# Attention with a routed expert layer: raw q, k in idle weight buffers, loads two iterations sooner, a third batch's choice on GpSimd

## The chip, the cores and the metric

The kernel runs on one core of one Trainium2 chip. The metric is device time in microseconds (us). Three runs of the kernel before gave 502.47, 502.87 and 504.84; the median is 502.87.

## The reference, cut to what matters

```python
# q, k, v: [4 batches, 12 heads, 448 rows, 64]
scores = q @ k.T / sqrt(64);  scores = where(row < col, -1e9, scores)
attn = softmax(scores);  x = (attn @ v), rearranged to [1792 tokens, 768]
logits = x @ w_gate + modality_bias[modality_id]          # 8 experts
e = argmax(logits, axis=1);  gate = softmax(logits)[e]
out[token] = gate * (relu(x[token] @ w1[e]) @ w2[e])       # w1 768x1024, w2 1024x768
```

All of it is float32. The expert of a token is chosen by its logits, so attention is computed nearly exactly: a float32 operand is split into a high part (rounded to the matmul's format) and a low part (the rest), and products are summed from the parts.

## The kernel before, in words

The program has one instruction stream per engine, written out in a fixed order. Each engine runs its stream in order, and waits at an instruction until what it needs is there. All plain transfers are issued by the sync engine (SP), also in order; GpSimd (POOL) issues the indirect ones. So the order of the text is the order in each queue.

**Attention** is a software pipeline over 48 heads (`iteration(n)`, L1079, n = 0 to 47). In iteration n TensorE (PE) makes the scores of head n (`st_scores`, banks `sa` and `sb`, one set), transposes the probabilities of head n-2, multiplies those of head n-3 with v (bank `ot`, one) and combines four earlier heads (bank `x`). VectorE (DVE) first adds the output of head n-4 (`ut`, L365), then normalises rows (`ltp`, L412, and `row`, L422), reads the scores of head n (`p`, L280), and last makes the low part `pl` (L321) of the transposed head n-2. ScalarE (ACT) does the exponentials (L290), the high part `ph` (L320), and copies. The next scores can only start when DVE has read the banks of the last, and the next product with v when DVE has done `ut` and `pl`.

**Raw q, k.** Two heads form a pair m. `load_qk(m)` loads 448 KB of raw q and k; POOL makes the high and low parts (`split_qk`, L194 and L195, in iteration 2m-4; `split_kl`, L200 and L202, in iteration 2m-3); SP moves them into stacked operands with four transfers (`stack_qk`, L211 and L212, iteration 2m-3); PE uses them from iteration 2m on. Before, the raw tile comes from a pool of two buffers, and the load stands at the end of iteration 2m-6. Pairs 0 to 2 are loaded whole at the start into parts of the six weight buffers `raw1[0..5]` (`first_view`).

**Rows and routing.** The normalised rows of a batch lie in four `row` buffers (one for each of four row tiles of 64, 128, 128 and 128 rows) and are stored to DRAM (`x_store`, L434). After a batch's last group (iterations 19, 31, 43 for batches 0 to 2) `after_batch` puts its routing into later iterations: `logits` and `top` on DVE, `ties` (L460 to L462), `first_tie` (L465, DVE), `choice` (L469, L470), `places` on PE, ranks, and four indirect writes of eight bytes per token into tables (L501, POOL). `ties` and `choice` are on POOL for batches 0 and 1, on DVE for 2 and 3. `later(n, f)` runs f after the scores of iteration n, `before(n, f)` ahead of them, `soon(n, f)` after the transposes.

**The first expert block.** From the counts of two batches the fullest expert is chosen (`first_slot`, iteration 38). In iterations 42 and 43 SP reads the tokens' ids from the tables (`pre_ids`, L718, four transfers each); `fetch_x` (L728, L729 on DVE, then the gather L730 on POOL) stands behind the scores of iterations 44 and 45. Its six weight blocks (512 KB each) are loaded by `start_w1` (L665) in iterations 42, 43, 44, 45, 46, 46, and POOL splits three of them in iterations 45 to 47 (`w1_chunk`, L673 and L674), after each of which SP loads a block of w2 into the same buffer.

**The expert layer** follows, with PE on matmuls nearly all of the time (L749 to L751).

Of the kernel before, what the change touches and what calls it, by code (L numbers as in the profile page):

```python
# [21 lines left out]
def attention_moe(  # L22
# [162 lines left out]

    def load_qk(m):
        b, j = divmod(m, H // 2)
        raw[m] = t = R([128, 2, S], F32, "raw")
        nc.sync.dma_start(out=t, in_=qk[b, j])

    def split_qk(m):
# [27 lines left out]
        stk.append([t[:, a] for a in range(2)])  # L219

    def first_view(m, c):
        k = 3 * m + c
        return raw1[k % K1][:, k // K1 * S:k // K1 * S + S]

    def first_load(m):
        nc.sync.dma_start(out=first_view(m, 2), in_=qk[0, m, :, 1])
# [154 lines left out]
    def st_comb(gr, i, x=None):  # L381
        b, u = divmod(gr, NG)
        q0, n = QT[i]
        if u == 0:
            xrow[b, i] = row()
            if i == 0:
                lt_all[b] = lts[b % 2]
                P.tensor_scalar(
                    out=lts[b % 2][:, :, H, :], in0=mb[:, b], scalar1=1.0, scalar2=0.0, op0=ALU.mult, op1=ALU.add
                )  # L390
        if x is None:
            x = bank("x")
        for j in range(GH // 2):
            nc.tensor.matmul(
                x[:, j * 2 * XW:(j + 1) * 2 * XW], lhsT=ots(gr, j)[:, q0:q0 + 128],
                rhs=wi[:, u * (GH // 2) + j].rearrange("p a c -> p (a c)"), start=True, stop=True,
            )
        cx[gr, i] = V, x
# [41 lines left out]

    def route(b):
        lg = sm([128, NTL, E], "lg")
        G = V if b >= B - 2 else P
        m = sm([128, NTL], "m")
        m2 = sm([128, NTL], "m2")
        oh = sm([128, NTL, E], "oh", BF16)
        pe = pes[b % 2]
        pc = sm([128, NP + E], "pc")
        sl = sls[b % 2]
        si = sm([128, NTL], "si", I32)  # L450
        zs = sm([128, NTL], "zs")

        def logits():
            V.tensor_reduce(out=lg, in_=lt_all.pop(b).rearrange("p t h e -> p t e h"), axis=AX, op=ALU.add)

        def top():
            V.tensor_reduce(out=m, in_=lg, axis=AX, op=ALU.max)

        def ties():
            G.tensor_tensor(out=lg, in0=lg, in1=wide(m), op=ALU.subtract)  # L460
            G.tensor_scalar(out=eq[:, :, 0:E], in0=lg, scalar1=0.0, scalar2=0.0, op0=ALU.is_equal, op1=ALU.add)
            G.tensor_tensor(out=eq[:, :, 0:E], in0=eq[:, :, 0:E], in1=e8v, op=ALU.mult)  # L462

        def first_tie():
            V.tensor_reduce(out=m2, in_=eq, axis=AX, op=ALU.max)  # L465

        def choice():
            ev = eq[:, :, 0:E]
            G.tensor_tensor(out=ev, in0=ev, in1=wide(m2), op=ALU.subtract)  # L469
            G.tensor_scalar(out=oh, in0=ev, scalar1=0.0, scalar2=0.0, op0=ALU.is_equal, op1=ALU.add)  # L470

        def places():
            prev = rt[b - 1][0][:, NP:] if b else ebase
            ohf = oh.rearrange("p t e -> p (t e)")
            pos = bank("x")
            nc.tensor.matmul(
                pos[:, 0:NP + E].rearrange("p (t e) -> p t e", e=E), lhsT=onesf,
                rhs=eb(prev, NTL + 1)[0:1], start=True, stop=False,
            )
            nc.tensor.matmul(pos[:, 0:NP], lhsT=upper, rhs=ohf, start=False, stop=False)  # L480
            for j in range(1, NTL + 1):
                nc.tensor.matmul(
                    pos[:, j * E:NP + E], lhsT=ones, rhs=ohf[:, 0:NP + E - j * E], start=False, stop=(j == NTL)
                )
            A.activation(out=pc, in_=pos[:, 0:NP + E], func=AF.Copy)
            A.activation(out=pe[:, :, 0:E], in_=lg, func=AF.Exp)
            rt[b] = (pc, si)

        def slots():
            G.tensor_tensor(  # L490
                out=sl[:, :, 0:E], in0=pc[:, 0:NP].rearrange("p (t e) -> p t e", e=E), in1=oh, op=ALU.mult
            )
            V.tensor_reduce(out=zs, in_=pe, axis=AX, op=ALU.add)

        def ranks():
            V.tensor_reduce(out=si, in_=sl, axis=AX, op=ALU.max)
            V.reciprocal(out=ent[:, b, :, 1].bitcast(F32), in_=zs)

        def scatter(ts=range(NTL)):
            for i in ts:  # L500
                P.indirect_dma_start(  # L501
                    out=tables[i][:, :], out_offset=bass.IndirectOffsetOnAxis(ap=si[:, i:i + 1], axis=0),
                    in_=ent[:, b, i, :], in_offset=None, bounds_check=NROW - 1, oob_is_err=False,
                )

        choose = ((1, logits), (1, top), (2, ties), (-3, first_tie), (3, choice))
        return choose, places, (slots, ranks), scatter

    def eb(a, x):
# [365 lines left out]
    with tc.manual_schedule():  # L875
        for m in range(2):
            first_load(m)
        load_v(0)
        first_load(2)
        nc.sync.dma_start(out=modi, in_=mod)  # L880
        nc.sync.dma_start(
            out=bias_sb.rearrange("p m o e -> p (m o e)"),
# [67 lines left out]
        def later(n, f):  # L950
            todo.setdefault(n, []).append(f)
# [62 lines left out]
                    P.tensor_tensor(out=mbv, in0=mbv, in1=mbt, op=ALU.add)  # L1014

        e0 = []
        W1AT = (11, 12, 13, 14, 15, 15)

        def start_w1(k):
            if k == 0:  # L1020
# [6 lines left out]
        def after_batch(b, n):  # L1027
            st = route(b)
            if b == B - 1:
                return st  # L1030
            choose, places, rank, scatter = st
            for j, f in choose:
                later(n + j, f) if j > 0 else before(n - j, f)
            last = b == B - 2
            soon(n + 4, places)
            for j, f in enumerate(rank, 1):
                (later if j % 2 else before)(n + 5 + j // 2, f)
            for i in range(NTL):
                later(n + 7 + (2 * i, i // 2, 0)[b], lambda i=i: scatter([i]))
            if b == 1:  # L1040
                later(n + 6, first_expert)
                before(n + 7, first_slot)
                for j, f in enumerate((first_shift, first_base, first_tri, first_order)):
                    later(n + 9 + j, f)
                for t in range(NPRE):
                    later(n + 11 + t, lambda t=t: pre_ids(t))
                    later(n + 13 + t, lambda t=t: fetch_x(0, 2 * S, t))
                for k in range(K1):
                    later(n + W1AT[k], lambda k=k: start_w1(k))

# [28 lines left out]
        def iteration(n):  # L1079
            if n % 2 == 1 and 5 < n + 3 < NHEAD:  # L1080
                stack_qk((n + 3) // 2)
            if n == 1:
                load_v(1)
            if n and n % GH == 0 and n // GH + 1 < B * NG:
                load_v(n // GH + 1)
            gr, i = divmod(n - 2 * GH, GH)
            comb = 0 <= gr < B * NG
            if 0 <= n - 4 < NHEAD:
                st_out(n - 4)
            if comb:  # L1090
                st_move(gr, i)
                st_norm(gr, i)
                b, u = divmod(gr, NG)
                if u == NG - 1:
                    later(n + 1, lambda i=i: x_store(b, i))
                    if i == NTL - 1:
                        after_batch(b, n)
            run_todo((n,))
            if n in (2, 3):
                st_trans(n - 2)  # L1100
            if n < NHEAD:
                st_scores(n)
            run_todo(n)
            if n == 0:
                split_vh(0)
                split_vl(0)
            if n % 2 == 1 and 5 < n + 3 < NHEAD:
                split_kl((n + 3) // 2)
            if n % 2 == 0 and 5 < n + 4 < NHEAD:
                split_qk((n + 4) // 2)  # L1110
            if n % GH == 1 and n > GH:
                st_sums(n // GH - 1, P)
            if n % GH == RECAT and n > GH:
                st_rec(n // GH - 1)
            if 0 <= n - 1 < NHEAD:
                st_exp(n - 1)
            if 0 <= n - 2 < NHEAD:
                if n > 3:
                    st_trans(n - 2)
                run_todo(-n)  # L1120
                st_split(n - 2)
            if 0 <= n - 3 < NHEAD:
                st_pv(n - 3)
                st_low(n - 3)
            gr, i = divmod(n - 2 * GH + 1, GH)
            if 0 <= gr < B * NG:
                st_comb(gr, i)
            if n % GH == 2 and n // GH + 1 < B * NG:
                split_vh(n // GH + 1)
                split_vl(n // GH + 1)  # L1130
            if n % 2 == 0 and n + 6 < NHEAD:
                load_qk((n + 6) // 2)

        for n in range(NHEAD):
            iteration(n)
# [285 lines left out]
```

## Time and profile before

| | |
|---|---|
| median of three runs | 502.87 us |
| profiled execution: its own time, its span | 505.04 us, 502.9 us |
| PE, PEld, DVE, ACT, POOL busy | 473.2, 445.3, 290.1, 276.8, 243.1 us |
| mean granted TensorE clock | 0.98 |
| DMA | 78.91 MB, mean 157 GB/s |
| chain that ended last, by engine | PE 51%, POOL 17%, DMA 9%, DVE 9%, issue 7%, ACT 4% |

The span is what the profile shows from first to last instruction; the own time of that execution is 2.14 us longer. Attention takes about the first 205 us, the expert layer the rest. In the profile's page PE is busy at 8 tenths or more of every slice, but the clock it was granted dips in slices of the attention part, and DVE, ACT and POOL, lightly used in the expert layer, are at 8 or 9 tenths there.

### The profile page before, as it was taken

To read this page: it belongs to the slowest core of one execution; us is meant where nothing else is said; L and a number is where in the kernel's file an instruction comes from. 1 tells how busy PE (TensorE), PEld (TensorE's weight loads), DVE (VectorE), ACT (ScalarE), POOL (GpSimd) and SP (SyncE) were. 2 spreads that over 40 slices of the span, in tenths; PEclk is the share of its full clock that TensorE was granted. 3 is DMA by queue.
4 is the path that set the end of the run, shared out by engine and by line. 5 is a ranking of instruction groups with operands and counts; after the bars stand their busy time and mean duration, and the time that the engine had idled before them with its cause. 6 is when DMAs were issued, how large, how long until landed. Compare 5 with 4: busy or idle time off the path is not lost.

```text
span 502.9 us, 10244 instructions
## 1 busy us (share of the span) xinstructions
PE 473.2 (94%) x3307; PEld 445.3 (89%) x3307; DVE 290.1 (58%) x863; ACT 276.8 (55%) x680; POOL 243.1 (48%) x327
## 2 busy tenths in 40 slices
PE   8999899999899977999999999999999999999991
PEld 6799899989798976878999999999999999889770
DVE  5899899989889967887512026442011120184490
ACT  6799899989798964616222116432112211284670
POOL 8999999899999898661221102202001001021131
PEclk9999999999899987999999999999999999999997
DMA  7787799987987689374496302872101001076300
GB/s 186 217 217 206 196 227 281 251 215 203 286 203 196 121 219 355 132 143 65 96 344 259 93 33 76 295 259 75 55 1 53 33 2 63 33 267 180 122 13 7
DMA packets 43816, 78.91 MB, mean 157 GB/s; under 512 B 15582, under 2 KB 27614, under 8 KB 43744
## 3 DMA queue, kind: packets, MB, share of 16 engines
q1 hardware_dynamic: 40624, 66.94, 48.3%
q0 software_dynamic: 3040, 11.03, 6.4%
q8 instruction: 28, 0.46, 0.4%
q14 instruction: 44, 0.36, 0.3%
q10 hardware_dynamic: 80, 0.11, 0.1%
HBM read 48.10 MB, written 11.89 MB: 119 GB/s over the span
## 4 chain that ended last, share of the span: by engine, by line
PE 51%; POOL 17%; DMA 9%; DVE 9%; issue 7%; ACT 4%; SPq 2%; POOLq 0%; DVEq 0%; ACTq 0%
PE g L751 7%; PE g L749 7%; PE g L750 7%; POOL vhl L247 3%; DMA table<-ent,si 3%; DMA idq<-table 2%; DMA st<-hl 2%; POOL hl L195 2%; POOL hl L194 2%; DVE pl L321 2%; PE ot L750 2%; PE x L751 2%; PE ot L749 2%; PE ot L751 2%; PE x L750 2%
## 5 line engine op out<-in xcount | busy, mean ns | idle before, releaser
L730 POOL DMA_INDIRECT xg<-xs,idg x18 | 21.0, 1166 | 157.1 <-DVEq L1331 79.9
L290 ACT ACTIVATE p<-p,nm 128x448 f32<-128x448 f32 x192 | 94.9, 498 | 2.4 <-DVE nm L280 2.4
L768 DVE SCALAR_TENSOR_TENSOR htl<-g,hth 128x256 fp32r<-128x256 f32 x40 | 16.7, 424 | 104.6 <-ACT hth L767 104.6
L749 PE MATMUL g<-xh,w1h 128*128 128x256 f32 x240 | 67.1, 279 | 0.4 <-DVE htl L768 0.4
L751 PE MATMUL g<-xh,w1l 128*128 128x256 f32 x240 | 67.2, 280 | 0.0
L750 PE MATMUL g<-xl,w1h 128*128 128x256 f32 x240 | 67.0, 279 | 0.0
L321 DVE TENSOR_TENSOR pl<-pt,ph 128x1024 fp32r<-128x1024 f32 x48 | 58.4, 1216 | 7.9 <-ACT ph L320 7.4
L302 PE MATMUL pt<-ident,p 128*128 128x128 f32 x480 | 61.6, 276 | 0.0
L334 PE MATMUL ot<-ph,vhl 128*128 128x448 f32 x192 | 50.6, 304 | 8.0 <-DVE ut L365 8.0
L302 PEld LDWEIGHTS pt<-ident,p 128*128 128x128 f32 x480 | 56.9, 143 | 1.2
L320 ACT ACTIVATE ph<-pt 128x1024 fp32r<-128x1024 f32 x48 | 49.1, 1024 | 11.8 <-PE pt L302 10.8
L767 ACT ACTIVATE hth<-g 128x256 fp32r<-128x256 f32 x40 | 15.1, 383 | 63.5 <-PE g L751 60.6
L749 PEld LDWEIGHTS g<-xh,w1h 128*128 128x128 f32 x240 | 44.9, 187 | 0.6 <-DVE htl L768 0.6
L809 POOL DMA_INDIRECT out_dram<-row,idg x14 | 16.7, 1190 | 59.5 <-ACTq L1315 33.5
L750 PEld LDWEIGHTS g<-xl,w1h 128*128 128x128 f32 x240 | 45.1, 188 | 0.0
L751 PEld LDWEIGHTS g<-xh,w1l 128*128 128x128 f32 x240 | 45.1, 188 | 0.0
L334 PEld LDWEIGHTS ot<-ph,vhl 128*128 128x128 f32 x192 | 33.4, 193 | 10.0 <-DVE ut L365 8.5
L280 DVE CUSTOM_DVE_ANT_0 p<-sa,mask 128x448 f32<-128x448 f32 x96 | 36.1, 412 | 4.8 <-PE sa L270 4.5
L290 ACT ACTIVATION_READ_ACCUMULATOR p<-p,nm 128x1 f32 x192 | 36.6, 191 | 0.0
L280 DVE CUSTOM_DVE_ANT_0 p<-sb,mask 128x192 f32<-128x192 f32 x96 | 36.3, 411 | 0.0
L341 PE MATMUL ot<-pl,vhl 128*64 128x64 f32 x192 | 35.1, 298 | 0.9 <-DVE pl L321 0.9
L359 ACT ACTIVATE hol<-ot 64x448 f32<-64x448 f32 x48 | 26.1, 543 | 15.8 <-PE ot L334 11.2
(363 smaller groups left out, 1306.7 us busy)
## 6 DMA issues: line engine op xcount, KB each, us to landing
st<-hl SPq DMA_DIRECT2D x56, 224.0 KB
raw<-in_moe_w_dram SPq DMA_DIRECT2D x24, 512.0 KB
raw<-in_qk_dram SPq DMA_DIRECT2D x21, 448.0 KB
raw<-in_moe_w_dram SPq DMA_DIRECT2D x20, 384.0 KB
vraw<-in_v_dram SPq DMA_DIRECT2D x12, 384.0 KB
xs<-row SPq DMA_DIRECT2D x12, 384.0 KB
w1h<-hl SPq DMA_DIRECT2D x14, 224.0 KB
w1l<-hl SPq DMA_DIRECT2D x14, 224.0 KB
```

The source lines that it names most:

```text
L280: V.tensor_tensor_reduce(out=z, in0=o, in1=m, scale=-scale, scalar=3.0e38, op0=ALU.add, op1=ALU.min, accum_out=nm[:n, i:i + 1],)
L290: A.activation(out=z, in_=z, func=AF.Exp, bias=nm[:n, i:i + 1], scale=-1.0, accum_out=sums[:n, b, i, h:h + 1],)
L302: nc.tensor.transpose(out=o, in_=a, identity=i)
L320: A.activation(out=ph, in_=t, func=AF.Copy)
L321: V.tensor_tensor(out=pl, in0=t, in1=ph.bitcast(F32), op=ALU.subtract)
L334: nc.tensor.matmul(o[:, q0:S], lhsT=t[:rows, kt, h].rearrange("p a d -> p (a d)"), rhs=ph[:rows, c0:c1], start=(n == 0), stop=(n == 1),)
L341: nc.tensor.matmul(o[0:D, q0:S], lhsT=t[:rows, kt, h, 0], rhs=pl[:rows, c0:c1], start=False, stop=False)
L359: A.activation(out=t, in_=ov[g][64:128, :S], func=AF.Copy)
L730: P.indirect_dma_start(out=xg[u][:n], out_offset=None, in_=xs[0:rows, :], in_offset=bass.IndirectOffsetOnAxis(ap=g[:n, 0:1], axis=0), boun ...
L749: nc.tensor.matmul(o, lhsT=ah, rhs=bh, start=first, stop=False)
L750: nc.tensor.matmul(o, lhsT=ah, rhs=bl, start=False, stop=False)
L751: nc.tensor.matmul(o, lhsT=al, rhs=bh, start=False, stop=last)
```

## The change

The raw tile of pair m is now a view of `raw1[5]`, `raw1[3]` or `raw1[4]` (by m mod 3), so there are three raw buffers instead of two. The views of pairs 0 to 2 are rearranged to leave these buffers early. `load_qk` stands two iterations sooner (end of iteration 2m-8; pair 3 in the opening, pairs 4 and 5 in iterations 1 and 3). Every third row tile of batches 0 to 2 gets one of two further buffers `xr`, so batch 3's first four tiles meet `row` buffers that were last used earlier. Batch 2's `ties` and `choice` go to POOL, one iteration sooner for `ties` and `first_tie`, and `choice` ahead of the scores of iteration 46. `fetch_x` of the first block stands ahead of the scores of iterations 45 and 46 instead of behind those of 44 and 45. The weight blocks are loaded in iterations 40, 42, 43, 44, 45, 46.

```diff
     def load_qk(m):
         b, j = divmod(m, H // 2)
-        raw[m] = t = R([128, 2, S], F32, "raw")
+        raw[m] = t = stack_view(raw1[(5, 3, 4)[m % 3]])
         nc.sync.dma_start(out=t, in_=qk[b, j])
...
     def first_view(m, c):
-        k = 3 * m + c
-        return raw1[k % K1][:, k // K1 * S:k // K1 * S + S]
+        k, j = (((3, 0), (3, 1), (4, 0)), ((2, 0), (2, 1), (4, 1)), ((0, 0), (0, 1), (1, 0)))[m][c]
+        return raw1[k][:, j * S:(j + 1) * S]
...
-            xrow[b, i] = row()
+            xrow[b, i] = T([128, DM], F32, "xr", 2) if b < B - 1 and (NTL * b + i) % 3 == 2 else row()
...
     def route(b):
-        G = V if b >= B - 2 else P
+        G = V if b == B - 1 else P
...
         def slots():
-            G.tensor_tensor(
+            (V if b >= B - 2 else P).tensor_tensor(
...
         choose = ((1, logits), (1, top), (2, ties), (-3, first_tie), (3, choice))
+        if b == B - 2:
+            choose = ((1, logits), (1, top), (1, ties), (2, first_tie), (-3, choice))
...
         first_load(2)
+        load_qk(3)
         nc.sync.dma_start(out=modi, in_=mod)
...
-        W1AT = (11, 12, 13, 14, 15, 15)
+        W1AT = (9, 11, 12, 13, 14, 15)
...
-                    later(n + 13 + t, lambda t=t: fetch_x(0, 2 * S, t))
+                    before(n + 14 + t, lambda t=t: fetch_x(0, 2 * S, t))
...
-            if n % 2 == 0 and n + 6 < NHEAD:
-                load_qk((n + 6) // 2)
+            if n in (1, 3):
+                load_qk(4 + n // 2)
+            if n % 2 == 0 and n > 3 and n + 8 < NHEAD:
+                load_qk((n + 8) // 2)
```

## Rows read from the trace of the kernel before

**Rows 1.** Stretches of ten us, 240 to 500: sum and mean of busy time.
```profile
sum 260.00, PE 250.95 PEld 239.39 DVE 84.23 ACT 87.62 POOL 40.39; mean PE 9.65 PEld 9.21 DVE 3.24 ACT 3.37 POOL 1.55
```
**Rows 2.** Timeline, ACT's high part `ph`: start, duration, instruction, [idle before <- releaser].
```profile
166.97 1.03 ACT L320 ACTIVATE ph<-pt 128x1024 fp32r<-128x1024 f32 x1 [0.46 <-PE pt L302]
170.56 1.03 ACT L320 ACTIVATE ph<-pt 128x1024 fp32r<-128x1024 f32 x1
174.46 1.01 ACT L320 ACTIVATE ph<-pt 128x1024 fp32r<-128x1024 f32 x1
182.67 1.03 ACT L320 ACTIVATE ph<-pt 128x1024 fp32r<-128x1024 f32 x1 [4.68 <-PE pt L302]
```
**Rows 3.** Timeline, 168 to 182, all engines: the first of the two late stalls.
```profile
168.78 0.33 SPq L189 DMA_DIRECT2D raw<-in_qk_dram  x1
...
172.23 0.77 SPq L212 DMA_DIRECT2D st<-hl  x1
...
176.42 0.94 POOL L194 TENSOR_SCALAR hl<-raw 128x896 fp32r<-128x896 f32 x1 [1.66 <-DMA raw<-in_qk_dram]
...
178.63 0.68 PE L270 MATMUL sa<-st 128*128 128x448 f32 x1 [3.04 <-DMA st<-hl]
...
180.66 0.42 DVE L422 TENSOR_TENSOR row<-x,rec 64x256 f32<-64x256 f32 x1 [3.32 <-DMA xs<-row]
...
181.99 0.24 POOL L412 TENSOR_TENSOR ltp<-cxt,rec 128x32 f32<-128x32 f32 x1
```
**Rows 4.** Timeline, 184 to 201, all engines: the second late stall.
```profile
184.69 3.04 SPq L718 DMA_DIRECT2D idq<-table  x4
...
190.82 0.16 DVE L728 TENSOR_REDUCE idg<-idq 128x1 int32<-128x4 int32 x1 [3.30 <-DMA idq<-table]
...
193.30 0.90 PE L334 MATMUL ot<-ph,vhl 128*128 128x448 f32 x2 [3.39 <-DVE ut L365]
...
193.80 0.61 DVE L280 CUSTOM_DVE_ANT_0 p<-sa,mask 128x448 f32<-128x448 f32 x1
...
200.33 0.54 PE L334 MATMUL ot<-ph,vhl 128*128 128x448 f32 x2
```
**Rows 5.** Stretches: PE, PEld, DVE, ACT, POOL busy, granted clock, DMA share, GB/s.
```profile
55.00:60.00 5.00, 3.48 (x30) 3.43 (x30) 3.06 (x13) 2.84 (x10) 4.92 (x6) 1.00 0.56 187
...
135.00:140.00 5.00, 5.00 (x33) 4.85 (x32) 3.91 (x16) 3.26 (x11) 4.74 (x8) 0.73 0.99 295
...
195.00:200.00 5.00, 5.00 (x26) 4.70 (x25) 4.79 (x15) 2.92 (x10) 4.07 (x5) 0.59 1.01 367
```
**Rows 6.** DMA rate from 168 to 178 in forty slices, GB/s.
```profile
GB/s 0 0 0 0 0 0 0 186 14 0 14 0 0 0 0 43 129 158 100 57 29 72 14 57 57 301 387 430 337 151 179 222 229 251 229 244 222 215 222 215
```
**Rows 7.** Timeline: two PE stalls earlier in attention, and DVE ahead of one.
```profile
56.52 0.47 PE L270 MATMUL sa<-xl,qz 128*128 128x448 f32 x1 [1.98 <-POOL qz L202]
...
130.23 0.93 DVE L454 TENSOR_REDUCE lg<-ltp 128x32 f32<-128x416 f32 x1 [1.57 <-POOL ltp L412]
...
133.21 0.56 PE L334 MATMUL ot<-ph,vhl 128*128 128x448 f32 x2 [2.13 <-DVE ut L365]
```
**Rows 8.** Timeline, POOL: batch 1's ties; the first block's split; the second gather.
```profile
136.64 0.24 POOL L460 TENSOR_TENSOR lg<-lg,m 128x32 f32<-128x32 f32 x1
...
137.59 1.14 POOL L200 TENSOR_TENSOR xh<-raw,hl 128x448 fp32r<-128x448 f32 x1
...
188.44 2.37 POOL L674 TENSOR_TENSOR w1l<-raw,w1h 128x1024 fp32r<-128x1024 f32 x1
...
191.25 1.07 POOL L730 DMA_INDIRECT xg<-xs,idg  x1 [0.44 <-DVE lg L460]
```
**Rows 9.** Timeline: a choice on DVE in batch 2 and batch 3, POOL beside the first.
```profile
193.81 2.37 POOL L674 TENSOR_TENSOR w1l<-raw,w1h 128x1024 fp32r<-128x1024 f32 x1
...
195.18 1.06 DVE L469 TENSOR_TENSOR eq<-eq,m 128x32 f32<-128x32 f32 x1
...
219.65 0.19 DVE L469 TENSOR_TENSOR eq<-eq,m 128x32 f32<-128x32 f32 x1
```

## The prediction

> **What bounds the kernel now.** I began with the sums by stretch. In the expert layer PE is busy 250.95 of 260 us [rows 1], and most of the missing 9.05 us is the end of the program; there PE's own work sets the time, and whatever attention ends earlier moves all of it. Attention is where four engines are level, so I took its beat next. ACT's `ph` comes every 3.59 us (166.97 to 170.56), 3.90 where a row tile is copied too (to 174.46) [rows 2]. A longer distance is a stall, and its excess is what can be won there. Two stalls near the end of attention are the largest.
>
> The first: from 174.46 to 182.67 are 8.21 us, 4.62 too many [rows 2]. PE waits 3.04 us for the stacked operands of pair 22 (`st`); the raw load of pair 23, issued at 168.78 just ahead of them, landed so late that POOL too lost 1.66 us; DVE then waits 3.32 us for a `row` buffer whose store stands in the queue behind these transfers [rows 3].
>
> The second: DVE stands 3.30 us in front of `idg`, because the ids of the second gather (four transfers, the last issued at 184.69 + 3.04 = 187.73) are there only at 190.82. Behind it in DVE's order is the `pl` of head 43, and behind that the `ut` of head 42, for which PE waits 3.39 us until 193.30 [rows 4]. After that PE's matmuls are slow: the granted clock is 0.59 in 195 to 200 [rows 5], a mixture of 1.2 and 2.4 GHz, and the next product with v comes at 200.33, 7.03 us later instead of 3.59 [rows 4]. So the second stall costs 3.39 + 3.44 = 6.83 us. Both together: 11.45 us.
>
> **The change part by part.** Heads and iterations are counted from 0; times are those of the profiled execution.
>
> *Raw loads two iterations sooner, in three buffers.* In the middle of attention each load keeps its place in SP's order (end of an even iteration) and its wait (the split of the iteration before); only the pair is another. I cost that at nothing; POOL hides it, since it is occupied between the loads. At the end pair 23 is loaded in iteration 38, and nothing of q, k is issued in 40. POOL's wait of 1.66 us goes.
>
> *Weight block 0 in iteration 40.* It takes the place in front of pair 22's `st` transfers that the raw load leaves, but earlier, behind the scores. The raw load moved almost nothing until 174.25, then 301 to 430 GB/s for one us [rows 6]. The `st` transfers were issued until 172.23 + 0.77 = 173.00 [rows 3]. Their landing, bounded from both sides: by the ids, which took 3.1 us from last issue to use [rows 4], 176.1; if block 0 is stuck as the raw load was, then 64 KB more, some 0.3 us at 187 to 387 GB/s, so 178.9. I take 176.5, near the lower end, because from 168 to 169.5 nothing was in motion [rows 6] and block 0 can use that. PE, idle from 178.63 - 3.04 = 175.59, then loses 0.9 instead of 3.04 us, with ends at 0.5 and 3.3. The Trainium skill, "DMA: Bandwidth & Descriptors", section "Queues, rings and completion order", says that a DMA engine serves the queues it has work for in turn, packet by packet; so indirect writes of POOL's queue could not hold a load of SP for long, and `st` would be there by 176.1. The gap in rows 9 speaks against it, without showing whose packets were stuck.
>
> *Two more row buffers.* Batch 3's tile 0 now reuses the buffer of batch 1's tile 2, stored long before. The 3.32 us on DVE go. What is late next is the batch-2 `logits` (L454), which need POOL's last `ltp`: POOL has it at 181.99 + 0.24 [rows 3], less the 1.66 us, so 180.6. Batch 1 shows such a wait of 1.57 us at 130.23, and PE then lost 2.13 us [rows 7]. So of the first stall's 4.62 us I count 2.1 as won on PE up to here; that POOL sets the pace keeps the rest.
>
> *Choice of batch 2 on POOL.* On POOL the three `ties` of batch 1 occupy 137.59 - 136.64 = 0.95 us with their gaps [rows 8]; the two of `choice` I put at two thirds, 0.63. Weight block 0's split ended at 188.44 + 2.37 = 190.81 [rows 8]; it now ends at 190.81 - 1.66 + 0.95 = 190.1. Behind it come the gather (1.07 [rows 8]) and `choice`, so about 192, before PE gets to `places` (194, below): not on the path. DVE loses five small instructions, 0.19 us each by batch 3's [rows 9], so 0.95. I count none of it, because the ids set DVE's time here. One of the five took 1.06 us, at 195.18, and ended at 196.24, just when POOL's split at 193.81 did (196.18) [rows 9]. The Trainium skill, "SBUF — State Buffer", section "Who interferes with whom", has it that a VectorE instruction with two SBUF inputs and a GpSimd instruction that reads SBUF shut each other out for a whole instruction. The trace agrees; by that rule DVE would save 1.8 instead of 0.95 us, and the sum below would not move.
>
> *`fetch_x` in front of the scores of iterations 45 and 46.* It is the main term. DVE now does `pl` of head 43, `ut` of head 42 and a row tile first, so PE's 3.39 us go. The ids are issued behind the same transfers; SP has no raw wait and one register read fewer ahead, which I put at 0 to 1 us, so they land between 189.8 and 190.8; I take 190.3. DVE comes to them about 188.3 and waits 2 us. What stands behind it now is `p` of head 46, at 190.3 + 0.3 = 190.6 instead of 193.80 [rows 4]: 3.2 us won. PE needs it for the scores of head 47. PE ended its transposes at 193.30 - 3.39 = 189.91; less 2.1 it is 187.8. Product and combination are 10 of an iteration's 28 matmuls and the longer ones, by my estimate 1.5 of the 3.59 us, which brings it to 189.3. It waits until `p` has read the first bank, 190.6 + 0.6 = 191.2: 1.9 us. If the first stall isn't mended, PE comes at 191.4 and waits for nothing. So the ids set the end in either case.
>
> *The clock.* After PE's stall of 1.98 us at 56.52 [rows 7] the clock was 1.00 (55 to 60); after 2.13 us at 133.21 it was 0.73 (135 to 140) [rows 5]. My 1.9 is nearest the first. At 2.4 GHz, from 191.2: scores and transposes 2.1 (the rest of the 3.59), 0.7 because `p` holds the second bank, 0.6 for `places` (estimates), so the product with v at 194.6 instead of 200.33: **5.7 us won**, of which 3.2 is the wait and 2.5 the clock.
>
> *The rest.* Pair 3 in the opening puts three small loads 0.6 us later, of which the first use is iterations away. Blocks 3 and 4 come an iteration sooner. A 512 KB block at the 387 to 430 GB/s of rows 9 is 1.2 to 1.4 us of the DMA engines; so each order could cost or give that much, and I take 0, since POOL splits them later than they land. Behind attention POOL is ahead of PE only by some us less than before, but the first product to need block 2 is far off.
>
> **The sum.** 505.04 (span 502.9 and 2.14 around it) - 5.7 = 499.3. That execution lies 2.17 above the median. If the 2.17 is in these very stalls, the median run wins 3.5 and comes to 499.3; if it is elsewhere, 497.2. I take **498.3**, with 496 to 500.5 as its own range.
>
> **Rivals.**
>
> *Both stalls go whole.* If the ids land by 188.3 and POOL's `ltp` isn't awaited, all 11.45 us go: 493.6, or 491.4 below the median's difference. For: each stall's named cause is moved. Against: no transfer ahead of the ids is taken out, and POOL has hardly a gap.
>
> *The stall returns at head 47.* If the ids take until 190.8 or the first stall is mended better, PE waits over 2.1 us for `p` of head 46, as at 133.21, and the clock falls: 3.44 us come back, 5.7 - 3.4 = 2.3 are left: 502.7, or 500.5 for the median.
>
> *Slower: late ids block the scores.* The two reads now stand in front of `p` of head 46, which frees both score banks, where before they held only `pl`. Place: DVE, iteration 46. It decides at 193.80 - 0.3 = 193.5; each later us costs a us, with PE's slow stretch as before. At 196, 2.5 us: 507.5, or 505.4. For: DMA is fully busy (1.01 in 195 to 200 [rows 5]). Against: nothing new stands ahead of the ids.
>
> *It doesn't do what it says:* the stalls of this execution aren't typical, or return elsewhere; 502 to 503.5.
>
> **How the numbers follow.** Forecast 0.52, both whole 0.13, stall at head 47 0.18, slower 0.09, no effect 0.08. What a measurement of this kernel tells from no change is about 0.5%, 2.5 us. Faster by more: 0.49 of the forecast, 0.13, and 0.05 of the third, 0.67. Slower: 0.09 and 0.01, 0.10. The same: 0.23. The range takes in the stall at head 47 and no effect, and the upper part of "both whole": 494 to 503.5.
>
> **What would show it.** In the changed profile: no wait of DVE for `xs<-row`; no wait of POOL for raw; PE's wait for `st` in the scores of head 44 under 1.5 us; `pl` of head 43 no longer behind `idg`; a wait of DVE of some 2 us for the ids in front of `p` of head 46; clock 1.00 from there on; the product with v of head 44 some 5 us behind that of head 43, instead of 7.03, at full clock. The prediction is wrong if the ids land past 193, if the clock falls once more between heads 44 and 47, or if PE gets idle time in the expert layer that it doesn't have now.

## The result, and the profile after

The changed kernel takes 497.88 us (median of 4 runs, 497.28 to 498.88) against 503.31 for the kernel before on the same chip (4 runs, 502.47 to 504.84): a ratio of 0.988 as recorded (the two medians give 0.989), 95% interval 0.985 to 0.991. The forecast was 498.3 with 494.0 to 503.5. Its profiled execution took 498.88 us with a span of 496.8; before it was 505.04 and 502.9.

Size and direction came out as forecast; three terms of the sum did not. The row of ACT's `ph` shows where (timeline of after; start, duration, instruction, [idle before <- releaser]; it answers to [rows 2]):

```profile
165.58 1.03 ACT L320 ACTIVATE ph<-pt 128x1024 fp32r<-128x1024 f32 x1
169.40 1.03 ACT L320 ACTIVATE ph<-pt 128x1024 fp32r<-128x1024 f32 x1 [0.26 <-PE pt L302]
173.30 1.01 ACT L320 ACTIVATE ph<-pt 128x1024 fp32r<-128x1024 f32 x1
177.71 1.03 ACT L320 ACTIVATE ph<-pt 128x1024 fp32r<-128x1024 f32 x1 [0.87 <-PE pt L302]
181.34 1.02 ACT L320 ACTIVATE ph<-pt 128x1024 fp32r<-128x1024 f32 x1
187.50 1.03 ACT L320 ACTIVATE ph<-pt 128x1024 fp32r<-128x1024 f32 x1 [1.12 <-PE pt L302]
192.38 1.02 ACT L320 ACTIVATE ph<-pt 128x1024 fp32r<-128x1024 f32 x1
```

Against before, 173.30 is 1.16 us ahead of 174.46, 177.71 is 4.96 ahead of 182.67 [rows 2]: the 8.21 us of the first stall have become 4.41. Part of that is lost again in the next long distance, from 181.34 to 187.50. Of the second stall about 2 us are left: the products with v of heads 43 and 44 (182.57 to 187.22 to 191.98, below) come 4.65 and 4.76 us behind the one before, where the beat is 3.6 to 3.9 and the second took 7.03 before [rows 4]. (On the page of the kernel before PE is busy at 7 tenths in the two slices from 176 to 201 us, where both stalls lie, and not at 8 or more as in the others but the last.)

The first stall after (timeline, all engines; it answers to [rows 3]):

```profile
164.12 0.36 SPq L667 DMA_DIRECT2D raw<-in_moe_w_dram  x1
...
171.18 0.62 SPq L212 DMA_DIRECT2D st<-hl  x1
...
173.67 0.94 POOL L194 TENSOR_SCALAR hl<-raw 128x896 fp32r<-128x896 f32 x1
...
175.28 0.44 PE L270 MATMUL sa<-st 128*128 128x448 f32 x1 [0.76 <-DMA st<-hl]
...
176.10 0.41 DVE L422 TENSOR_TENSOR row<-x,rec 64x256 f32<-64x256 f32 x1
...
179.28 0.24 POOL L412 TENSOR_TENSOR ltp<-cxt,rec 128x32 f32<-128x32 f32 x1
...
179.55 0.96 DVE L454 TENSOR_REDUCE lg<-ltp 128x32 f32<-128x416 f32 x1 [1.67 <-POOL ltp L412]
...
182.57 0.56 PE L334 MATMUL ot<-ph,vhl 128*128 128x448 f32 x2 [1.26 <-DVE ut L365]
```

POOL's wait for raw and DVE's wait for the `row` buffer no longer stand there, PE waits 0.76 us for `st` instead of 3.04. What is late next is POOL's `ltp`, 1.67 us for DVE.

The second stall after (timeline, all engines; it answers to [rows 4]):

```profile
182.31 2.00 SPq L720 DMA_DIRECT2D idq<-table  x4
...
187.03 0.16 DVE L730 TENSOR_REDUCE idg<-idq 128x1 int32<-128x4 int32 x1 [0.28 <-DMA idq<-table]
...
187.18 0.61 DVE L280 CUSTOM_DVE_ANT_0 p<-sa,mask 128x448 f32<-128x448 f32 x1
...
187.22 0.54 PE L334 MATMUL ot<-ph,vhl 128*128 128x448 f32 x2
...
191.86 0.18 PE L480 MATMUL x<-oh,upper 128*128 128x32 bf16 x1 [0.42 <-POOL oh L470]
191.98 0.53 PE L334 MATMUL ot<-ph,vhl 128*128 128x448 f32 x2
```

DVE stands 0.28 us for the ids, not the 2 us forecast, and PE waits for none of it. The product with v of head 44 comes at 191.98; before it was 200.33 [rows 4], so 8.35 us are won up to here, 2.65 more than the 5.7 of the forecast. Of these, 1.16 were there at 173.30 already, ahead of both stalls; the two stalls gave 7.19. The span gained only 6.1, so 2.25 us were given back later. Here is where (timeline, all engines, behind attention):

```profile
205.89 2.38 POOL L676 TENSOR_TENSOR w1l<-raw,w1h 128x1024 fp32r<-128x1024 f32 x1
...
206.83 2.26 DVE L679 TENSOR_TENSOR w2l<-raw,w2h 128x768 fp32r<-128x768 f32 x1
...
208.23 0.95 POOL L412 TENSOR_TENSOR ltp<-cxt,rec 128x32 f32<-128x32 f32 x1
...
213.21 0.38 PE L476 MATMUL x<-pc,onesf 1*128 1x40 f32 x2 [1.61 <-DVE row L422]
...
215.23 0.95 DVE L679 TENSOR_TENSOR w2l<-raw,w2h 128x768 fp32r<-128x768 f32 x1
```

The split of w2 on DVE took 2.26 us beside POOL's split of w1; by itself the same instruction takes 0.95 (at 215.23). It stands in front of the last batch's choice and the row tile behind that, for which PE then waits 1.61 us before `places`, and in this execution the clock falls (stretches of after: PE, PEld, DVE, ACT, POOL busy, granted clock, DMA share, GB/s; the first answers to the last of [rows 5]):

```profile
195.00:200.00 5.00, 4.49 (x33) 3.82 (x31) 4.47 (x9) 3.73 (x8) 4.92 (x6) 1.00 0.81 290
...
210.00:215.00 5.00, 3.39 (x19) 2.44 (x18) 3.96 (x17) 1.05 (x3) 4.07 (x5) 0.93 0.99 311
215.00:220.00 5.00, 5.00 (x18) 4.00 (x17) 4.55 (x23) 0.00 (x0) 0.22 (x1) 0.73 1.02 136
```

In the kernel before that `places` product (L476) is at 220.52, so 7.31 of the 8.35 us were left at 213.21. Behind it came the slow stretch, which the kernel before does not have there (1.00 from 215 to 225).

### The profile page after: what moved, and what is told of

It reads as the page before. It is cut to its first block, busy times and chain, and to the rows that moved or that the text cites. A ratio compares the mean times of both kernels' runs of the same rounds, so it can differ in the third digit from the quotient of the medians.

```text
span 496.8 us, 10248 instructions
## 1 busy us (share of the span) xinstructions
PE 470.7 (95%) x3307; PEld 443.0 (89%) x3307; DVE 290.3 (58%) x858; ACT 276.4 (56%) x680; POOL 245.8 (49%) x332
## 5 line engine op out<-in xcount | busy, mean ns | idle before, releaser
L302 PE MATMUL pt<-ident,p 128*128 128x128 f32 x480 | 60.2, 273 | 0.0
L302 PEld LDWEIGHTS pt<-ident,p 128*128 128x128 f32 x480 | 55.3, 141 | 1.1
```

Of the source, the lines that this page charges most:

```text
L302: nc.tensor.transpose(out=o, in_=a, identity=i)
```

## The experiments

All were timed in five rounds beside the kernel before, which had medians of 503.28, 504.14 and 504.33 us in the three sessions. The kernel after was timed in another, so a difference of about 1 us from its median is weak by itself, and the traces have to carry it.

**Where does the gain come from? The reads back where they were.** The kernel after, with one line undone:

```
-  before(n + 14 + t, lambda t=t: fetch_x(0, 2 * S, t))
+  later(n + 13 + t, lambda t=t: fetch_x(0, 2 * S, t))
```

> The changed kernel with the two reads of ids (fetch_x) back behind the scores of iterations 44 and 45. Theory (the reads are the main term): the ids of the second gather land at about 187.0 as in the changed kernel, DVE stands for them from about 184.6 with first_tie and pl of head 43 behind, PE loses some 2.5 us there and perhaps the clock once: 3 to 5 us slower than the changed kernel, 501 to 503. Rival (earlier raw loads and the choice on GpSimd make the gain): at most 1 us slower, 498 to 499.

Measured: 500.0 us (498.98 to 500.62), ratio 0.993 (0.991 to 0.995), 2.1 above the kernel after: less than the 3 to 5 of the theory, more than the 1 of the rival. The second stall is back with the old releasers (timeline, DVE and PE):

```profile
187.77 0.16 DVE L730 TENSOR_REDUCE idg<-idq 128x1 int32<-128x4 int32 x1 [3.16 <-DMA idq<-table]
...
189.80 0.56 PE L334 MATMUL ot<-ph,vhl 128*128 128x448 f32 x2 [2.08 <-DVE ut L365]
```

The clock in 190 to 195 is 0.66. So the order of the reads is worth about 2 us in the time once the rest is there, less than the 5.7 that the prediction hung on it. The 2 us are not the reads' alone: attention ends 3.8 us later in this profile (last `ph` at 202.07 against 198.30), of which 2.2 are lost in the first stall (6.61 us from `ph` to `ph`; PE waits 2.06 us at 176.39), ahead of the moved reads; and behind attention nothing is given back (`places` at 215.97 waits 0.59 us, clock 1.00). The ids land at 187.77 here too: their coming 3 us sooner than before is not the moved reads' doing.

**The reads alone**, the same line put the other way into the kernel before.

> The kernel before with only the reads of ids moved in front of the scores of iterations 45 and 46. Theory: the first late stall stays, the second goes; the ids land near 190.8 as before, p of head 46 follows at 191.1 instead of 193.8 and the half-clock stretch goes: 4 to 6 us faster than before, 497.5 to 499.5. Rival (the ids land earlier only because of the other edits, so that nothing is won by the order alone): within 1.5 us of before.

Measured: 503.94 us, ratio 1.001 (0.999 to 1.003). My theory fell: nothing is won. DVE no longer waits for the ids, yet PE waits 3.21 us for `ut` at 192.21, almost as before (timeline, DVE and POOL):

```profile
186.84 1.17 DVE L460 TENSOR_TENSOR lg<-lg,m 128x32 f32<-128x32 f32 x1
186.91 1.06 POOL L673 TENSOR_SCALAR w1h<-raw 128x1024 fp32r<-128x1024 f32 x1
...
188.06 2.39 POOL L674 TENSOR_TENSOR w1l<-raw,w1h 128x1024 fp32r<-128x1024 f32 x1
188.27 2.23 DVE L462 TENSOR_TENSOR eq<-eq,e8v 128x32 f32<-128x32 f32 x1
...
190.42 1.21 DVE L321 TENSOR_TENSOR pl<-pt,ph 128x1024 fp32r<-128x1024 f32 x1
```

Two `ties` of 128x32, 0.18 and 0.19 us in the kernel before (at 190.96 and 191.40), take 1.17 and 2.23 us and end within 0.1 us of POOL's splits (187.97 and 190.45). In the kernel before, the ids held both engines up; now DVE's small instructions run into POOL's large ones.

**The choice back on DVE**, in the kernel after:

```
-  G = V if b == B - 1 else P
+  G = V if b >= B - 2 else P
...
-  if b == B - 2:
-      choose = ((1, logits), (1, top), (1, ties), (2, first_tie), (-3, choice))
```

> The changed kernel with batch 2's ties and choice on DVE again, in the iterations of before. Theory (DVE has room there once the reads are moved, and GpSimd is what is late behind attention): within 1 us of the changed kernel, rather faster, 496.5 to 498.5. Rival (the choice on GpSimd is what relieves DVE): 1.5 to 3 us slower, 499.5 to 501.

Measured: 498.98 us, ratio 0.991 (0.989 to 0.994), 1.1 above the kernel after: my theory (within 1 us, rather faster) missed, and the rival's 1.5 to 3 us were not reached. The `ties` on DVE wait out POOL's splits again, and PE waits for the `ut` behind them (timeline, DVE, POOL and PE):

```profile
183.88 1.24 DVE L460 TENSOR_TENSOR lg<-lg,m 128x32 f32<-128x32 f32 x1
184.01 1.06 POOL L673 TENSOR_SCALAR w1h<-raw 128x1024 fp32r<-128x1024 f32 x1
...
185.15 2.39 POOL L674 TENSOR_TENSOR w1l<-raw,w1h 128x1024 fp32r<-128x1024 f32 x1
185.37 2.23 DVE L462 TENSOR_TENSOR eq<-eq,e8v 128x32 f32<-128x32 f32 x1
...
189.31 0.56 PE L334 MATMUL ot<-ph,vhl 128*128 128x448 f32 x2 [3.27 <-DVE ut L365]
```

The clock in 190 to 195 is 0.66. From `ph` to `ph` it is 9.56 us (186.07 to 195.63) instead of 4.88. So the edit that the prediction costed at nothing is worth over 3 us in its place (195.63 against 192.38); but only 1.1 is left in the time: behind attention POOL has gaps here (it waits 1.94 us for ACT's copy) and the split of w2 takes its 0.95, so the kernel with the choice on DVE gives nothing back there.

**Is it POOL's split, or just five more instructions on DVE?** The kernel just named, with the splits of blocks 0 to 2 two iterations later:

```
-  later(NHEAD - KA + k, lambda k=k: w1_chunk(k, P))
+  later(NHEAD - 1 + k, lambda k=k: w1_chunk(k, P))
```

> The kernel after with batch 2's choice on DVE again, and POOL's splits of w1 blocks 0 to 2 put two iterations later, so that POOL reads no large tile while DVE does ties and choice. Theory (DVE's small instructions with POOL's split beside them wait for its end): the ties' L462 takes about 0.2 us instead of 2.23, L469 0.2 instead of 1.02, L460 0.2 instead of 1.24, the longest wait of PE for ut there is under 1.5 us instead of 3.3, and the clock stays at 0.9 or more in 190 to 195 instead of 0.66; what POOL does later may cost as much behind attention, so the total says little (496 to 504). Rival (five more instructions on DVE are what costs, POOL's split has nothing to do with it): L462 stays at 2 us or PE's wait at 3 us.

Measured: 511.18 us, ratio 1.013 (1.010 to 1.017), beyond the 496 to 504 expected: behind attention PE now waits 5.4 us for the late low parts and 3.3 for the high parts. But in the place asked about, the instructions on DVE (timeline) are:

```profile
184.21 0.18 DVE L460 TENSOR_TENSOR lg<-lg,m 128x32 f32<-128x32 f32 x1
184.42 0.21 DVE L461 TENSOR_SCALAR eq<-lg 128x32 f32<-128x32 f32 x1
184.66 0.19 DVE L462 TENSOR_TENSOR eq<-eq,e8v 128x32 f32<-128x32 f32 x1
...
190.14 0.24 DVE L469 TENSOR_TENSOR eq<-eq,m 128x32 f32<-128x32 f32 x1
```

All are short, PE waits for no `ut` between 184 and 196, and the clock in 190 to 195 is 1.00 (DVE does wait 1.58 us for the ids, at 188.53). The rival falls: L460 to L462 in the same order take 0.58 us without POOL's split beside them and 3.65 with it (1.24 + 0.18 + 2.23). The Trainium skill, "SBUF — State Buffer", section "Who interferes with whom", says that a VectorE instruction with two SBUF inputs and a GpSimd instruction that reads SBUF exclude each other for a whole instruction; these runs agree.

**Reads and choice together, in the kernel before.** If those two were the whole of it, this would win.

> The kernel before with two edits of the change: fetch_x in front of the scores, and batch 2's choice on POOL; raw loads, row buffers and W1AT as before. Theory (the two edits win only together: with the reads moved, DVE's ties and choice run into POOL's w1 splits, and the choice on POOL takes them away): 4 us faster than before, 498.5 to 500.5; ties (L462) on DVE gone, PE's wait for ut behind it under 1.5 us, clock 0.9 or more in 190 to 200; the first stall (about 8 us from ph to ph near 175 to 183) still there. Rival (the reads need the first stall mended too, because the ids land behind the late transfers): 502 to 504, with a wait of DVE for the ids of 2 us or more.

Measured: 503.57 us, ratio 1.000 (0.998 to 1.002). My theory fell again, and the rival that came nearer in time named the wrong wait. With the ties gone, DVE comes sooner to a row tile and finds no buffer (timeline, DVE and PE):

```profile
178.02 0.42 DVE L422 TENSOR_TENSOR row<-x,rec 64x256 f32<-64x256 f32 x1 [2.64 <-DMA xs<-row]
...
192.13 0.42 DVE L422 TENSOR_TENSOR row<-x,rec 128x256 f32<-128x256 f32 x1 [5.53 <-DMA xs<-row]
192.48 0.15 DVE L730 TENSOR_REDUCE idg<-idq 128x1 int32<-128x4 int32 x1
...
192.70 1.30 PE L394 MATMUL x<-wi,ut 128*128 128x144 f32 x4 [4.89 <-DVE idg L731]
```

Four row buffers hold up two tiles of batch 3, not one. The second wait is, by the order of the buffers, for batch 2's tile 2, which SP stores only behind the second gather's ids (186.06 in this run). It was hidden before: DVE came to that tile at 193.36, after its wait for the ids.

**Two row buffers fewer**, in the kernel after (`row()` in place of the `"xr"` tile).

> The kernel after without the two more row buffers. Theory: DVE waits 2 to 3.3 us for xs<-row of batch 3's tile 0 again, the first stall returns in part: 1 to 3 us slower than the kernel after, 499 to 501. Rival (the store is early enough now that the transfers ahead of it are earlier, or POOL's ltp sets the pace in any case): within 0.7 us of the kernel after.

Measured: 499.68 us, ratio 0.993 (0.990 to 0.995), 1.8 above the kernel after. The size is as expected, the place is not: DVE's wait at tile 0 is 0.60 us, and the one that costs is the second (timeline, DVE):

```profile
176.04 0.42 DVE L422 TENSOR_TENSOR row<-x,rec 64x256 f32<-64x256 f32 x1 [0.60 <-DMA xs<-row]
...
189.36 0.42 DVE L422 TENSOR_TENSOR row<-x,rec 128x256 f32<-128x256 f32 x1 [3.69 <-DMA xs<-row]
```

**Raw loads late**, at their old iterations but still in w1 buffers:

```
-  if n in (1, 3):
-      load_qk(4 + n // 2)
-  if n % 2 == 0 and n > 3 and n + 8 < NHEAD:
-      load_qk((n + 8) // 2)
+  if n % 2 == 0 and n + 6 < NHEAD:
+      load_qk((n + 6) // 2)
```

(`load_qk(3)` in the opening goes too.)

> The kernel after with the raw loads of q, k at their old iterations (still in the idle w1 buffers). Theory: at the end pair 23's load lies again in front of pair 22's stacked operands, with block 0 ahead of it, so PE waits 2 to 4 us for st and POOL about 1.5 us for raw, and the distance from ph to ph there is over 7 us: 2 to 3 us slower than the kernel after, 500 to 501. Rival (the loads land in time wherever they stand, or the later stall takes up what is lost): at most 1 us slower.

Measured: 500.42 us, ratio 0.993 (0.990 to 0.997), 2.5 above the kernel after, but its runs lie far apart (498.23 to 502.81, and one of 506.86 that is not in the ratio), and in the profiled one attention ends only 1.5 us later (last `ph` at 199.78 against 198.30). PE waits 2.47 us for `st`, POOL 1.48 for raw, and from `ph` to `ph` it is 7.71 us. That the loads stood in front of pair 22's operands was right: in the four profiles with late raw loads PE waits 2.31 to 3.04 us for `st` there, in the eight with early ones at most 0.76, except for the 2.06 of the reads put back.

**The w1 loads at their old iterations** (11, 12, 13, 14, 15, 15).

> The kernel after with the w1 loads at their old iterations (11, 12, 13, 14, 15, 15). Theory (the order of the blocks costs and gives nothing, POOL splits them later than they land): within 0.8 us of the kernel after. Rival (block 0 earlier is what frees pair 22's stacked operands and the ids): 1.5 to 3 us slower, with PE waiting over 2 us for st.

Measured: 497.77 us, ratio 0.988 (0.985 to 0.991): the same as the kernel after. That part does nothing by itself.

**The give-back.** The kernel after, with the split of w2's first chunk behind the last choice:

```
-  w2_chunk(0)
   st_sums(g, V)
...
-  w2_chunk(1)
+  w2_chunk(0, 1)
```

> The changed kernel with the split of the first w2 block moved from in front of the last batch's sums and logits to behind its stores, beside the second block's. Theory (2.2 us are given back behind attention because DVE's w2l of 2.26 us, held up by GpSimd's split of weight block 5, stands in front of the last logits, PE then waits 1.61 us for the choice and its clock falls): 1.3 to 3 us faster than the changed kernel, 495 to 496.6, PE's wait at L476 under 0.6 us and no half clock in 214 to 220. Rival (GpSimd's own lateness, its last ltp, sets the last logits): within 0.7 us of the changed kernel.

Measured: 496.67 us (496.5 to 497.1), ratio 0.987 (0.984 to 0.989), 1.2 under the kernel after, and no run of the one overlaps the other's, though the intervals of the two ratios do. The chain behind attention is shorter now, 13.98 us from the last `ph` (197.76) to `places` instead of 14.91; before it was 13.86 (timeline, all engines):

```profile
205.35 2.37 POOL L676 TENSOR_TENSOR w1l<-raw,w1h 128x1024 fp32r<-128x1024 f32 x1
...
206.28 1.48 DVE L372 TENSOR_SCALAR rec<-sums 128x16 f32<-128x16 f32 x1
...
211.74 0.38 PE L476 MATMUL x<-pc,onesf 1*128 1x40 f32 x2 [0.72 <-DVE row L422]
```

PE's wait is 0.72 us, a little over the 0.6 expected. The clock in 210 to 220 is 1.00; but it is 1.00 too in the kernel with the w1 loads at their old iterations, which has the late split (2.26 us at 206.37) and a wait of 1.66 us at 212.77. So the slow stretch of the kernel after does not follow from the wait alone, and what it adds is not shown. Now L372 is what waits for POOL's split: 1.48 us, 0.168 by itself in the kernel before, and its end, 207.76, is POOL's, 207.72.

**A step further:** on top of that, in the last group of batches 0 to 2 the last row tile is scaled by DVE, so that `logits` need nothing of POOL:

```
-  if i == 3 or i == 1 and gr >= B * NG - 2:
+  if i == 3 and (gr % NG != NG - 1 or gr >= B * NG - 2) or i == 1 and gr >= B * NG - 2:
```

> The kernel with the first split of w2 moved behind the last choice (496.67), and besides the last row tile of each of batches 0 to 2 is scaled by DVE from PSUM instead of being copied by ACT and scaled by POOL. Theory (DVE's logits wait 1.6 to 1.7 us for POOL's ltp of that tile, PE then 2.1 and 1.8 us for ut, with half clock at 135 to 140): those waits go, DVE pays 0.6 us per tile: 1.5 to 4 us faster than that kernel, 492.5 to 495. Rival (DVE is the fuller engine there, and the 0.6 us comes back as a wait for p or ut): 496 to 498.

Measured: 495.9 us (494.34 to 499.28), ratio 0.985 (0.981 to 0.989), the fastest median here, though its runs overlap those of the last one: between the theory's 492.5 to 495 and the rival's 496 to 498. Both waits for `ltp` are gone. The clock in 130 to 140 is 1.00 (after: 0.74 and 0.92), but it is so in the kernel that this one builds on as well. Some of the gain comes back (timeline, PE):

```profile
182.83 0.44 PE L270 MATMUL sa<-st 128*128 128x448 f32 x1 [2.82 <-DVE pl L321]
```

The named `pl` had ended at 182.39, and the scores do not read it. These are the first scores with pair 23's stacked operands, which SP issued until 179.09. In the kernel after it issued them until 181.18 and PE used them at 185.07, with the transfer named as what it waited for. So it is probably the transfer here too.

## Why the prediction was right in size, and where not

- **The first stall.** `st` was put 0.9 us late and was 0.76 late (with ends of 0.5 and 3.3; in the kernel with the reads put back, the same code up to there, it was 2.06); the row wait and POOL's raw wait went; POOL's `ltp` was named as late next (forecast 180.6, measured 179.28 + 0.24 = 179.5). DVE waited 1.67 us for it, as batch 1 had led one to expect (1.57 [rows 7]). The rates and the gap that the prediction puts down to rows 9 are those of [rows 6].
- **The ids: mis-sized.** The step said "I put at 0 to 1 us, so they land between 189.8 and 190.8; I take 190.3". They were there at 187.03, 3.8 us sooner than before. Of these, 1.16 us were the lead at 173.30. SP began to issue them at 182.31 instead of 184.69, 2.38 sooner, and the issue itself took 2.00 instead of 3.04. In the kernel before SP had stood 2.2 us for the first stall's own transfers, by the releasers that the profile names (waits of SP in before, 174 to 184: who waited <- for what, us in total, times, longest); after, it names no transfer there:

```profile
SPq L434 <- DMA st<-hl: 0.7, 1, 0.7
SPq L718 <- DMA st<-hl: 0.6, 1, 0.6
SPq L211 <- DMA st<-hl: 0.5, 1, 0.5
SPq L718 <- DMA raw<-in_qk_dram: 0.4, 1, 0.4
```

  I had carried the first stall's repair over to PE and DVE, but to SP with 0 to 1 us only, and had written that the ids set the end in either case. The forecast's expected wait of 2 us in front of `p` of head 46 was 0.28, and the product with v of head 44 was at 191.98, not 194.6, though 4.76 us behind head 43's (187.22), as forecast (5).
- **The choice on POOL: "I count none of it, because the ids set DVE's time here."** With the ids early they did not. Without this edit the second stall comes back in another dress (9.56 us from `ph` to `ph`). The trace before held the hint, L469's 1.06 us [rows 9]; I weighed that rule for 0.85 us, and it bore on 3. Nor was the choice on POOL off the path: PE came to `places` at 191.03 instead of 194 and waited 0.42 us for its `oh` (191.86).
- **The row buffers.** The first wait was costed; the second was hidden behind the wait for the ids in the profile, and would have taken its place: 5.53 us with the first stall left, 3.69 without.
- **The clock** went as forecast from the first stall on: 1.00 from 170 to 210. The rule behind it, from the length of the wait, does not hold (last section).
- **"Behind attention POOL is ahead of PE only by some us less … far off": wrong.** 2.25 us were given back there. Not a product missed its block: DVE's split of w2 and POOL's of w1 now overlap and keep each other out. In the kernel before POOL's had ended 4 us ahead of DVE's (211.16 against 215.19), and POOL waited 2.57 us for ACT's copy until 213.73. Moving one of them won 1.2 us by the medians. PE's wait before `places`, 1.61 us instead of 0.59, is idle time of the kind that the prediction had named as a sign of being wrong.
- **The rivals.** The condition of "both stalls whole" (ids by 188.3, `ltp` not awaited) was met in its first half only. The stall did not return at head 47, late ids did not block the scores.
- **One execution.** Part of what the two profiles differ by is chance. In the reads-alone and the reads-and-choice kernels, whose raw loads and row buffers are those of before, the first stall is 5.93 and 5.97 us long (`ph` at 174.69 and 180.62, 172.49 and 178.46), not 8.21, with a clock of 1.00 from 175 to 185. The lead of 1.16 us at 173.30 is within the same spread: the second of these kernels, with the code of before up to there, is at 172.49.

So the total was met with luck, because errors cancel: the two stalls gave 1.49 us more than the 5.7 forecast, 1.16 were a lead from before them, and 2.25 came back behind attention. Taken one by one from the kernel after, the parts are worth 2.5 (raw loads), 2.1 (reads), 1.8 (buffers), 1.1 (choice) and 0 (w1 loads): 7.5 us, more than the 5.4 of the whole (medians of different sessions, over which the kernel before moved by 1 us). Reads and choice in the kernel before are worth 0. Each removes one of the waits that stand one behind the other in the same iterations, so the first two do not count while the others are there. What the raw loads or the buffers alone do in the kernel before was not run. That the w1 loads are not needed was shown only with the rest in place. Why the raw-late kernel's runs lie so far apart was not settled.

## What to carry to other kernels

When a wait is removed, list everything else that the waiting engine would meet in the next few us at its new, earlier time: buffers whose store is not yet out, and large instructions of the neighbour that it was kept apart from. And carry each repair through every queue, the issuing one too: the ids of the second stall were late in part because of the first.

## What the runs showed of the hardware

- The size of the shut-out. DVE instructions that take 0.17 to 0.24 us alone took 1.0 to 2.3 beside a GpSimd split of 1.05 or 2.4 us, and ended with it within 0.1 us. It also works the other way: POOL's `ltp` took 0.95 us instead of 0.24 beside DVE's split of w2. It isn't only for instructions with two inputs: `rec<-sums`, a TENSOR_SCALAR with one, took 1.48, in one run. The Trainium skill, "SBUF — State Buffer", section "Who interferes with whom", counts `tensor_scalar` among the operations that can take the shared ports, depending on their operands.
- The length of PE's last wait does not tell whether the clock falls. After 2.08 us (reads back) it was 0.66 in the next five us, after 2.02 (two buffers fewer, at 189.93) it stayed at 1.00, and after 2.31 (reads alone, at 178.19) it was 1.00 in 175 to 185. At one place of the code, PE's wait of 2.06 to 2.16 us for `ut` near 132, the five us from 130 or from 135 fell to 0.73 to 0.83 in four profiles (before, after, reads back, choice on DVE) and stayed at 1.00 in three (reads alone, reads and choice, w1 loads at their old iterations). The prediction's step from 1.98 and 2.13 us to a bound at about 2.1 was too neat.
